# Low parts of the last quad on GpSimd, and the loads of batch five moved, in a fused attention and two-layer mixing kernel

## The chip, the cores and the metric

The kernel runs on one core of a Trainium2 chip. The metric is the device time of one execution in microseconds (us). Engine names are those of the profile: PE (TensorE matmuls), PEld (its weight loads), ACT (ScalarE), DVE (VectorE), POOL (GpSimd), SP (SyncE, which only issues DMAs here). ACTq and SPq are the DMA queues of ACT and SP.

## What is computed

Batch 8, 8 heads, 576 tokens, head size 64, 32 memories per head; then two pairs of dense layers, over tokens (576 to 256 to 576) and over channels (512 to 1536 to 512).

```python
a = exp(phi - max(phi, axis=2)); a = a / (sum(a, axis=2) + 1e-9)
k_m = einsum('bhsm,bhsd->bhmd', a, k)
v_m = einsum('bhsm,bhsd->bhmd', a, v)
scores = q @ k_m.T / sqrt(64); scores = scores - max(scores)
attn = exp(scores); attn = attn / (sum(attn) + 1e-9)
x = concat_heads(attn @ v_m)                 # 8 x 576 x 512
h = relu(x.T @ w_tok1) @ w_tok2
u = x + h.T
out = u + relu(u @ w_ch1) @ w_ch2
```

## The kernel before

**Channel layers.** The 8 x 576 = 4608 rows of u are cut into nine chunks of 512 tokens, and the hidden layer into twelve blocks of 128. An operand is kept as a high part (a rounded cast on ACT) and a low part (what the cast left, a subtraction), and a product of two operands is three matmuls. Chunks 0 to 2 are plain (matmuls L161 and L184). Chunks 3 to 8 do the first layer with seven products of half size instead of eight (class Quarters; products qa and qb at L322, their combined weights loaded as `unit` at L392 on ACT's queue). For each pair of hidden blocks ACT copies products from PSUM into the tile `whole` (L1921), DVE adds them up (L1924), ACT and DVE make the high and low parts (L126, L129), and the second layer (acc, L184) of the pair before fills the gaps between the products. All products of a pair share two PSUM tiles, so the next product into qa waits until ACT has copied the last one out.

**Attention and token layers.** They run in quads, (b, Q) being four heads of batch b (class Quad, L399). A quad loads phi (L407), kv (L412, one buffer) and q (L417), makes the softmax over tokens (phi, with all-reduces over partitions on POOL at L432 and L454), the memories (L467; from (5, 0) on this is issued together with the quad before's scores), the scores (L566), their softmax S, writes S out to DRAM in another layout (`rows`, L663) and reads it back (`raw`, L670 for four full row blocks and L673 for the tail; the buffer is the one that the next quad's q takes). `nat_full` and `nat_tail` split raw into high and low parts (cast on ACT L122, subtraction on DVE L123), `step_A` (Ap, L708) and `step_R` (Rp, L727) are the first token layer, and `step_u` (u, L748) the second one together with attn @ v. For attn, `a_pair` casts a transposed S on ACT (L638) and subtracts on `low_eng` (L639): on POOL for batches 2 and 3, on DVE from batch 4 on. `v_pair` then writes vv on ACT (L652) into the buffer (`aT`) that those subtractions read.

**Order.** Batches 0 and 1 are arranged by a planner; its code is untouched by the change. From then on the order is a table of events written by hand: `at(h, fn)` (L1775) puts a step at a time h counted in half blocks of the channel layers, 24 per chunk, and `run` (L1877) issues it when the loops get there; `quarters` (L1903) has eight such points per pair of hidden blocks, half a unit apart. `starts` (L1779) lists for each quad the times m (memories) and r (scores): (4, 0) has m = 59 and r = 63.5, (4, 1) has 69 and 74, (5, 0) has 79 and 86. Every engine and every DMA queue works strictly in the order in which its instructions are issued.

**The start.** The first lines make an identity matrix on POOL (`make_identity`, masks.py:199 is its AFFINE_SELECT) and a mask (L90 to L95), then a small tile of zeros (L103) that ACT's first activation (L105) reads. PE's first matmuls (L1085) read the identity. Instructions named `ISA` in the order of POOL are of two kinds: those with operands are the all-reduces of L432 and L454, and one without operands stands ahead of every first instruction of another kind (ahead of masks.py:199, ahead of the first L432 after subtractions, ahead of the first L639 or L196 after all-reduces).

Of the kernel before, what the change touches and what calls it, by code (L numbers as in the profile page):

```python
# [28 lines left out]
def kernel(  # L29
# [30 lines left out]
    B, _, _, _, NC, _, D = kv.shape  # L60
# [5 lines left out]
    NF = 2 * w_ch2.shape[0]  # L66
# [1660 lines left out]
    for Q, h0 in ((0, 3), (1, 11)):  # L1727
        qd = quads[1, Q]
        late = 4 if not Q else 0
# [27 lines left out]
    for z in order:  # L1757
        if z.eng == "PE":
# [3 lines left out]
            if gap > 0.3 and z.take:  # L1762

                late = any(y.eng == "SP" and y.ready > z.begin - 0.5 for y in z.after)
# [10 lines left out]
    def at(h, fn, *x, k=0):  # L1775
        events.setdefault((max(h, 0), k), []).append((fn, x))

    JOINT = (4, 1)
    starts = [(2, 0, 24, 24), (2, 1, 34, 34), (3, 0, 38, 44), (3, 1, 49, 54), (4, 0, 59, 63.5), (4, 1, 69, 74)]  # L1779
    while starts[-1][:2] != (B - 1, 1):  # L1780
        b, Q, m, r = starts[-1]
        starts.append((b + Q, 1 - Q, r + 5, r + NF))
    for b, Q, m, r in starts:
        qd = second if b == 2 and not Q else Quad(b, Q)
        fine = b > 2
        if b > 3:
            qd.low_eng = nc.vector
        if qd is not second:
            at(max(m - (13 if JOINT < (b, Q) else 11), 2 * NF), qd.load_phi)
            if fine:  # L1790
                w = 1.5 * ((b, Q) == (5, 0))
                at(m - (6 if (b, Q) == (3, 0) else 8.5 - w), qd.phi_max, k=1)
                w += (b, Q) == (3, 0)
                w -= 1.5 * (JOINT < (b, Q))
                at(m - 4.5 + w, qd.phi_sub)
                at(m - 4 + w, qd.phi_only_exp)
                w += 1.5 * (JOINT < (b, Q))
                at(m - 3.5 + w, qd.phi_sum)
            else:
                at(m - 7, qd.phi_max, k=1)  # L1800
                at(m - 3, qd.phi_exp, k=1)
                at(m - 2, qd.phi_sum, k=1)
            at(loaded + (5 if (b, Q) > (3, 1) else 1), qd.load_kv, k=1)
            at(r - (3 if fine else 4), qd.load_q, k=1)
        joint = JOINT < (b, Q)
        if joint:
            former.follow, loaded = qd, m - 3
        else:
            at(m, qd.step_kv)
            loaded = m  # L1810
        qd.follow, former = None, qd
        at(r + 2, qd.step_s, k=int((b, Q) == (3, 0)))
        if fine:
            late = 0.5 * ((b, Q) == (4, 0))
            for x, fn in (
                (m + 0.5, qd.scales), (m + 1, qd.turn_keys), (m + 1.5, qd.spread_v),
                (m + 3.5, qd.get_keys), (m + 5, qd.v_high), (m + 6, qd.v_low),
                (r + 2.5, qd.S_max), (r + 3, qd.sub_exp), (r + 4, qd.S_sum), (r + 4.5, qd.S_mul),
                (r + 4.5, qd.rows_out), (r + 5, qd.turn_pairs), (r + 8 + late, qd.nat_full),
                (r + 8.5 + late, qd.nat_tail), (r + 9.5 + late, qd.step_A),  # L1820
                (r + 10.5 + late, qd.step_R),
            ):
                at(x, fn)
            at(r + 6, qd.rows_in, "qT", 1)
            for x in range(2):
                at(r + 6 + x / 2, qd.a_pair, x)
                at(r + 7 + x / 2, qd.v_pair, x)
            for x in range(4):
                k = int((b, Q, x) == (3, 1, 0))
                at(r + 12 + x // 2 * 1.5 + x % 2 / 2, qd.step_u, x // 2, x % 2, k=k)  # L1830
            continue
        at(m + 4, qd.values)
        at(m + 1, qd.step_T)
        at(r + 3, qd.sm2)
        at(r + (3 if qd is second else 4), qd.a_pair, 1)
        at(r + 6, qd.nat, k=1)
        at(r + 7, qd.v_pairs)
        at(r + 8, qd.step_A)
        at(r + 9, qd.step_R)
        for x in range(4):  # L1840
            at(r + 10 + x // 2 * (1 if qd is second else 2), qd.step_u, x // 2, x % 2)
    for c in range(2, CHUNKS):
        h = 2 * NF * (c - 1)
        at(h + (9 if c == 2 else 7 if c <= WIN else 1), lambda c=c: mixer(c).take(), k=1)
        if c < WIN:
# [3 lines left out]
        late = (  # L1849
            (-6.5, -3, -2.5, -6.5, -3, -2.5, -3.5, -1, -0.5, -1, -0.5, 0, 0.5)  # L1850
            if c > WIN
            else (-3.5, -3, -2.5, -3.5, -2, -3, -3, -2, -2.5, 0.5, 0.5, 1, 1)
        )
# [217 lines left out]
```

## Time and profile before

| what | value |
|---|---|
| three runs | 772.58, 772.42 and 772.87 us (median 772.58) |
| profiled execution | 773.63 us; its span 771.8 us, so 1.83 us lie outside the span |
| granted clock of TensorE, mean | 0.997 |
| PE busy | 750.7 us (97%), 5159 matmuls |
| DVE, ACT, POOL busy | 469.4 us (61%), 337.3 us (44%), 86.0 us (11%) |
| chain that ended last | PE 79%, DVE 7%, DMA 5%, issue 5% |
| SP's first nine loads | issued from 0.72 to 5.07 us |
| PE's waits from 312 to 330 us | 0.50 at 315.69, 0.54 at 318.64, 0.92 at 322.43, 0.19 at 325.02, 1.94 at 329.53 |

Times inside the profile count from the span's start. A busy PE says only that matmuls follow each other closely; the value in brackets behind an instruction is how long its engine sat idle before it, and which engine's or DMA's end released it. That idle time is shorter than the real gap between two instructions' starts would suggest, since the ends of pipelined matmuls are modelled.

### The profile page before, as it was taken

The numbers are of one execution on the slowest core, as the hardware profiler recorded it, in microseconds if no ns is written. First come the engines' busy times: TensorE is split into PE (matmuls) and PEld (weight loads), VectorE is DVE, ScalarE is ACT, GpSimd is POOL, SyncE is SP. The second block draws the span as 40 slices with busy tenths as digits, with TensorE's granted clock in tenths as the row PEclk, the third lists the DMA queues.
The fourth block names the chain that finished last, engine by engine and source line by source line (L and its number), as shares of the span: only waits on it lengthen the run. The fifth ranks groups of instructions, "written<-read, shape, count | busy, mean of one in ns | idle before, by whom it ended". The sixth has DMA issues, their size and how long they took to land.

```text
span 771.8 us, 13321 instructions
## 1 busy us (share of the span) xinstructions
PE 750.7 (97%) x5159; PEld 652.5 (85%) x5159; DVE 469.4 (61%) x892; ACT 337.3 (44%) x771; POOL 86.0 (11%) x78
## 2 busy tenths in 40 slices
PE   4999999999999999899999999999999999999998
PEld 4877888787888888779898889898989989889987
DVE  1889895577658666756585648674856245335224
ACT  2789663143323243525363536353635343333331
POOL 0224344010132023000000000000000000000000
PEclk9999999999999999999999999999999999999999
DMA  9756442374743554768486848785767356556651
GB/s 364 273 201 248 117 167 73 110 229 167 227 117 87 233 147 128 220 213 282 135 270 198 279 129 250 233 231 173 207 201 199 119 175 225 175 176 212 198 179 68
DMA packets 90446, 147.34 MB, mean 191 GB/s; under 512 B 41488, under 2 KB 60304, under 8 KB 86160
## 3 DMA queue, kind: packets, MB, share of 16 engines
q1 hardware_dynamic: 69216, 79.77, 31.5%
q10 hardware_dynamic: 21168, 66.73, 27.9%
q8 instruction: 41, 0.67, 0.3%
q14 instruction: 21, 0.17, 0.1%
HBM read 121.57 MB, written 24.90 MB: 190 GB/s over the span
## 4 chain that ended last, share of the span: by engine, by line
PE 79%; DVE 7%; DMA 5%; issue 5%; ACT 2%; POOL 1%; SPq 1%; ACTq 0%; POOLq 0%; DVEq 0%
PE acc L184 32%; PE qa L322 12%; PE qb L322 9%; PE cp L161 8%; PE u L748 7%; PE Ap L708 3%; DMA raw<-rows 2%; PE u L1406 2%; DMA rows<-S 2%; PE sp L566 1%; DMA kv<-in_kv_dram 1%; PE Rp L727 1%; PE sp L467 1%; DMA sums<-c1h 1%; PE end L184 1%
## 5 line engine op out<-in xcount | busy, mean ns | idle before, releaser
L184 PE MATMUL acc<-qhh,c 128*128 128x512 f32 x376 | 146.1, 396 | 0.0
L322 PEld LDWEIGHTS qb<-x,unit 128*128 128x128 f32 x648 | 92.2, 189 | 10.4 <-ACT whole L1921 0.9
L322 PEld LDWEIGHTS qa<-xT,unit 128*128 128x128 f32 x648 | 91.8, 188 | 9.5 <-issue 0.2
L184 PE MATMUL acc<-hh,c 128*128 128x512 f32 x288 | 96.5, 394 | 0.0
L322 PE MATMUL qb<-x,unit 128*128 128x256 f32 x648 | 94.7, 282 | 0.5 <-ACT whole L1921 0.5
L322 PE MATMUL qa<-xT,unit 128*128 128x256 f32 x648 | 94.3, 281 | 0.0
L1924 DVE TENSOR_TENSOR whole<-whole 128x256 f32<-128x256 f32 x72 | 30.4, 422 | 101.9 <-ACT whole L1921 101.7
L184 PEld LDWEIGHTS acc<-qhh,c 128*128 128x128 f32 x376 | 71.0, 189 | 12.4 <-issue 3.7
L1921 ACT COPY whole<-qa 128x256 f32<-128x256 f32 x108 | 40.1, 371 | 88.4 <-PE qa L322 84.8
L184 PE MATMUL acc<-qal,c 128*128 128x512 f32 x276 | 78.2, 394 | 0.0
L184 PE MATMUL acc<-qhl,c 128*128 128x512 f32 x188 | 74.9, 398 | 0.0
L184 PEld LDWEIGHTS acc<-hh,c 128*128 128x128 f32 x288 | 54.1, 188 | 13.9 <-issue 2.5
L184 PE MATMUL acc<-hl,c 128*128 128x512 f32 x144 | 56.2, 390 | 0.0
L1921 ACT COPY whole<-qb 128x256 f32<-128x256 f32 x72 | 26.6, 370 | 62.2 <-PE qb L322 62.2
L161 PE MATMUL cp<-uh,c1h 128*128 128x512 f32 x144 | 51.5, 398 | 0.0
L161 PE MATMUL cp<-ul,c1h 128*128 128x512 f32 x144 | 50.3, 390 | 0.0
L161 PE MATMUL cp<-uh,c1l 128*128 128x512 f32 x144 | 50.3, 390 | 0.0
L184 PEld LDWEIGHTS acc<-qal,c 128*128 128x128 f32 x276 | 46.2, 189 | 4.2
L129 DVE SCALAR_TENSOR_TENSOR hl<-cp,hh 128x512 fp32r<-128x512 f32 x36 | 24.7, 686 | 32.3 <-ACT hh L126 32.2
L129 DVE SCALAR_TENSOR_TENSOR qhl<-whole,qhh 128x256 fp32r<-128x256 f32 x72 | 30.4, 422 | 19.2 <-ACT qhh L126 18.4
L126 ACT ACTIVATE qhh<-whole 128x256 fp32r<-128x256 f32 x72 | 30.2, 419 | 25.6 <-DVE whole L1924 18.0
L184 PEld LDWEIGHTS acc<-qhl,c 128*128 128x128 f32 x188 | 36.1, 192 | 0.7
(239 smaller groups left out, 1431.0 us busy)
## 6 DMA issues: line engine op xcount, KB each, us to landing
unit<-sums ACTq DMA_DIRECT2D x108, 512.0 KB, 4.0
kv<-in_kv_dram SPq DMA_DIRECT2D x12, 1280.0 KB, 7.6
rawc<-in_w_ch_dram SPq DMA_DIRECT2D x12, 1024.0 KB, 7.2
q<-in_q_dram SPq DMA_DIRECT2D x16, 576.0 KB, 6.3
unit<-sums ACTq DMA_DIRECT2D x36, 256.0 KB, 3.4
sums<-sums SPq DMA_DIRECT2D x12, 512.0 KB, 6.2
phi<-in_phi_dram SPq DMA_DIRECT2D x16, 320.0 KB, 5.3
out_dram<-u SPq DMA_DIRECT2D x5, 1024.0 KB, 4.2
```

The costliest lines, as they stand in the source:

```text
L126: nc.scalar.activation(out=h, in_=ps, func=AF.Relu)
L129: nc.vector.scalar_tensor_tensor(out=l, in0=ps, scalar=0.0, in1=f32(h), op0=ALU.max, op1=ALU.subtract)
L161: nc.tensor.matmul(ps, l[:, a, w], r[:, a], start=n == 0, stop=n == len(mm) - 1)
L184: nc.tensor.matmul(ps, l_[f // 2][:, f % 2, a * P : (a + 1) * P], r[:, w], start=f == start and x == 0, stop=f == end - 1 and x == 2,)
L322: nc.tensor.matmul(ps[:, :HW], l, r, start=first and n == 0, stop=n == len(mm) - 1, skip_group_check=not first,)
L467: nc.tensor.matmul(s.kvp[32 * i : 32 * i + 32, : 2 * D], s.pt[:, i, j, :], s.kv[:, :, j, i, :], start=j == 0, stop=j == NC - 1,)
L566: nc.tensor.matmul(s.sp[hf][m, :HALF], s.kb[w, m], s.qT[w, i], start=True, stop=True)
L708: nc.tensor.matmul(ps[:, :TT], a, w, start=x == 0, stop=x == len(mm) - 1)
L748: nc.tensor.matmul(ps[:, :HALF], a, r, start=x == 0, stop=x == len(mm) - 1)
L1406: nc.tensor.matmul(ps[:, :HALF], a, r, start=n == 0, stop=n == len(mm) - 1)
L1921: nc.scalar.copy(out=to, in_=ps[:, :HW])
L1924: nc.vector.tensor_tensor(out=to, in0=x, in1=y, op=ALU.add)
```

## The change

Four edits of the event table:

- In the last quad (7, 1) `low_eng` stays POOL, so its two subtractions of L639 move from DVE to POOL.
- The half unit that put `nat_full`, `nat_tail`, `step_A` and `step_R` of quad (4, 0) later is dropped.
- `load_kv` of quad (5, 0) is issued three units after the memories of (4, 1), not five.
- `load_phi` of batch 5 is issued twelve units ahead of m, not thirteen.

```diff
-        if b > 3:
+        if b > 3 and (b, Q) != (B - 1, 1):
             qd.low_eng = nc.vector
         if qd is not second:
-            at(max(m - (13 if JOINT < (b, Q) else 11), 2 * NF), qd.load_phi)
+            at(max(m - (11 if (b, Q) <= JOINT else 12 if b == 5 else 13), 2 * NF), qd.load_phi)
...
-            at(loaded + (5 if (b, Q) > (3, 1) else 1), qd.load_kv, k=1)
+            at(loaded + (3 if (b, Q) == (5, 0) else 5 if b > 3 else 1), qd.load_kv, k=1)
...
         if fine:
-            late = 0.5 * ((b, Q) == (4, 0))
             for x, fn in (
...
-                (r + 4.5, qd.rows_out), (r + 5, qd.turn_pairs), (r + 8 + late, qd.nat_full),
-                (r + 8.5 + late, qd.nat_tail), (r + 9.5 + late, qd.step_A),
-                (r + 10.5 + late, qd.step_R),
+                (r + 4.5, qd.rows_out), (r + 5, qd.turn_pairs), (r + 8, qd.nat_full),
+                (r + 8.5, qd.nat_tail), (r + 9.5, qd.step_A), (r + 10.5, qd.step_R),
```

On ACT, around the token layer of quad (4, 0), the order before was this (names end in the head group and a running number; `whole<-qa` is the copy that frees the PSUM tile of the products qa):

```order
L652 CAST vv_0_3057<-vh_0_2793 64x128 x4
L392 DMA unit_3072<-sums_1326 128x512
L1921 COPY whole<-qa_3_3071 128x256
L122 CAST nat_0_3081<-raw_0_3011 128x512
L1921 COPY whole<-qb_3_3092 128x256
L122 CAST nat_0_3081<-raw_0_3011 64x128
```

With the change the same place on ACT reads (the copies of `whole` are L1919 now, since two lines are gone):

```order
L652 CAST vv_0_3057<-vh_0_2793 64x128 x4
L122 CAST nat_0_3066<-raw_0_3011 128x512
L392 DMA unit_3075<-sums_1326 128x512
L1919 COPY whole<-qa_3_3074 128x256
L122 CAST nat_0_3066<-raw_0_3011 64x128
L1919 COPY whole<-qb_3_3096 128x256
```

The cast of raw now stands ahead of a load of weights and of the copy that frees qa. On DVE the tail's subtraction moves along: it follows the subtraction of the full blocks directly, where a reduction of phi (L421), a residual addition (L202) and an addition of `whole` stood between them. On PE `step_A` stands one product and one group of second-layer matmuls earlier, and `step_R` one product earlier.

On SP's queue, from the keys of quad (4, 1) to the reading back of its rows, the difference is:

```order
 L519 DMA keys_1_3035<-T_1_3032 32x2x32 x4
 L417 DMA q_1_3064<-in_q_dram 128x1152
-L528 DMA kb_1_3103<-keys_1_3035 64x128 x2
-L412 DMA kv_0_3175<-in_kv_dram 128x2560
+L412 DMA kv_0_3090<-in_kv_dram 128x2560
+L528 DMA kb_1_3105<-keys_1_3035 64x128 x2
 L205 DMA out_dram<-o_2809 128x2048
-L407 DMA phi_1_3368<-in_phi_dram 128x640
-L663 DMA rows_1_3383<-S_1_3278 32x18x32 x4
+L663 DMA rows_1_3381<-S_1_3278 32x18x32 x4
+L407 DMA phi_1_3405<-in_phi_dram 128x640
```

The kv of quad (5, 0) goes ahead of two small loads of keys (kb), directly behind q; the phi of quad (5, 1) goes behind the four stores of rows of quad (4, 1) and so between them and the reading back of raw. The phi of (5, 0) keeps its place in the queue.

At the end of POOL's program the difference is:

```order
 L432 ISA prr_1_5483<-pr_1_5481 128x128
 L454 ISA psr_1_5673<-pr_1_5671 128x128
-L2064 UNCONDITIONAL_BRANCH
-L2064 ISA
+L639 ISA
+L639 TENSOR_TENSOR a_7_1_6291<-aT_1_6289,a_7_1_6291 64x576
+L639 TENSOR_TENSOR a_7_1_6292<-aT_1_6289,a_7_1_6292 64x576
+L2062 UNCONDITIONAL_BRANCH
+L2062 ISA
```

The last work of POOL is two subtractions, where it was an all-reduce, with an `ISA` without operands ahead of them.

## Rows read from the trace of the kernel before

**Rows 1.** Waits: engine and line, what it awaited; us in total, times, longest
```profile
PE pp L1085 <- POOL mask L91: 11.0, 1, 11.0
...
PE sp L467 <- DMA kv<-in_kv_dram: 1.9, 1, 1.9
```

**Rows 2.** Timeline of POOL: start, duration, line, operation, [idle before it, releaser]
```profile
10.66 0.28 POOL masks.py:199 TENSOR_SCALAR_AFFINE_SELECT ident<-ident 128x128 f32<-128x128 f32 x1 [9.74 <-issue]
...
273.79 3.80 POOL L639 TENSOR_TENSOR a<-aT,a 64x576 fp32r<-64x576 f32 x2 [15.46 <-ACT a L638]
...
291.30 5.58 POOL L196 TENSOR_TENSOR o<-uh,ul 128x512 f32<-128x512 f32 x4 [7.13 <-DMA kv<-in_kv_dram]
...
534.13 1.07 POOL L454 PARTITION_ALL_REDUCE psr<-pr  x1 [13.56 <-DMA unit<-sums]
```

**Rows 3.** Timeline of PE, the start
```profile
11.00 6.34 PE L1085 MATMUL pp<-ident 128*128 128x128 f32 x30 [11.00 <-POOL mask L91]
...
21.04 0.77 PE L1252 MATMUL kp<-kv,pt 128*32 128x64 f32 x40
```

**Rows 4.** Timeline of PE around quad (4,0)
```profile
312.21 0.87 PE L322 MATMUL qb<-x,unit 128*128 128x256 f32 x6
...
313.62 0.87 PE L322 MATMUL qa<-xT,unit 128*128 128x256 f32 x6
...
315.69 0.98 PE L322 MATMUL qb<-x,unit 128*128 128x256 f32 x6 [0.50 <-ACT whole L1921]
...
326.36 0.30 PE L748 MATMUL u<-a,vv 128*128 128x288 f32 x1
...
327.29 0.29 PE L748 MATMUL u<-w2h,Rl 128*128 128x288 f32 x1
...
329.53 1.30 PE L467 MATMUL sp<-kv,phi 128*32 128x128 f32 x40 [1.94 <-DMA kv<-in_kv_dram]
```

**Rows 5.** Timeline of ACT around quad (4,0)
```profile
311.95 0.37 ACT L1921 COPY whole<-qa 128x256 f32<-128x256 f32 x1
...
314.74 0.62 ACT L122 CAST nat<-raw 128x512 fp32r<-128x512 f32 x1 [2.42 <-DMA raw<-rows]
...
325.73 0.74 ACT L445 ACTIVATE phi<-phi 128x640 f32<-128x640 f32 x1 [0.91 <-DVE phi L435]
```

**Rows 6.** Timeline of SP's queue around quads (4,0) and (4,1)
```profile
318.61 0.35 SPq L417 DMA_DIRECT2D q<-in_q_dram  x1
...
320.34 0.53 SPq L412 DMA_DIRECT2D kv<-in_kv_dram  x1
...
344.28 2.34 SPq L663 DMA_DIRECT2D rows<-S  x4
```

**Rows 7.** Stretches of 2 us: busy time by engine, PEclk, DMA share, GB/s
```profile
330.00:332.00 2.00, 2.00 (x49) 0.89 (x40) 0.00 (x0) 0.00 (x0) 0.00 (x0) 0.69 1.01 416
...
332.00:334.00 2.00, 2.00 (x7) 1.71 (x8) 0.85 (x2) 0.00 (x0) 0.00 (x0) 0.50 0.55 208
```

**Rows 8.** Timeline of SP's queue, the start
```profile
2.10 0.43 SPq L1270 DMA_DIRECT2D kv<-in_kv_dram  x1
```

**Rows 9.** DMA issues, 0 to 24 us: KB each, median us to landing
```profile
kv<-in_kv_dram SPq DMA_DIRECT2D x2, 640.0 KB, 9.2
```

**Rows 10.** Timeline of DVE: quads (4,0), (4,1) and (7,1)
```profile
318.30 0.28 DVE L123 TENSOR_TENSOR nat<-raw,nat 64x128 fp32r<-64x128 f32 x1
...
355.33 1.35 DVE L421 TENSOR_REDUCE pr<-phi 128x128 f32<-128x640 f32 x1
...
589.42 0.75 DVE L639 TENSOR_TENSOR a<-aT,a 64x576 fp32r<-64x576 f32 x1 [1.32 <-ACT a L638]
```

**Rows 11.** The line that loads kv (L412), all twelve loads
```profile
DMA to landing us min/median/max: 5.5/7.6/9.1
```

**Rows 12.** Timeline of ACT, last quad (7,1)
```profile
591.97 0.59 ACT L652 CAST vv<-vh 64x128 fp32r<-64x128 f32 x2
```

**Rows 13.** The chain of waits, 300 to 345 us: start, us, what
```profile
309.65 5.06 DMA raw<-rows
```

## The prediction, made before the run

> **What bounds the kernel now.** I read the waits of the whole run first. PE is busy nearly throughout, so an edit is worth something only where PE itself stands still or runs slower. Two such places lie near the change. The first is the start: PE waits 11.0 us for POOL's mask [rows 1], and POOL's timeline shows why. Its first AFFINE_SELECT begins at 10.66 after 9.74 us in which POOL waited for nothing that the profile shows ("issue") [rows 2]; PE begins at 11.00 [rows 3]. The second is the memories of quad (5, 0): PE waits 1.94 us for kv [rows 1] before 329.53 [rows 4]. The timeline before that shows a row of shorter waits for ACT's copies and for nat; ACT waited 2.42 us for raw before the nat cast at 314.74 [rows 5], and SP issued q at 318.61 and kv only at 320.34 [rows 6]. Right after the wait the stretches 330 to 332 and 332 to 334 have a granted clock of 0.69 and 0.50, the latter being the lower of the clock's two levels, 1.2 GHz [rows 7].
>
> **The change part by part.** The sum is made against the profiled execution, 773.63 us (span 771.8 and 1.83 around it), which is 1.05 above the median of the runs, 772.58; I take the savings off both.
>
> *Last quad's subtractions, at the far end of the program: what POOL leaves behind.* The same unexplained gap appears inside the run. POOL goes from all-reduces back to tensor operations at 291.30 after 7.13 us of idle [rows 2], with a load of kv as releaser, which that addition does not read; I read it so that a change of the kind of operation costs POOL 7 us, and that at the start it asks for the tensor kind once more and loses 9.74. The last work of POOL before is an all-reduce at 534.13 [rows 2]; with the change it is a subtraction, the kind that the next execution begins with. If POOL keeps between executions what it last held, the next start finds it in place. Then POOL could do its AFFINE_SELECT about 9.7 sooner and PE begin at 1.4 instead of 11.0. Not all of it need arrive: the first kv is issued at 2.10 [rows 8] and lands 9.2 later [rows 9], at 11.3, while PE uses it at 21.04 [rows 3], which would be 11.4 with a gain of 9.6. That just fits, and the other early loads have a little more room. I take **-9.1**, bounds -9.6 and -7.5 (two us of late loads), if the gap goes at all. If POOL loads anew at every start, this term is 0; no row here shows what an execution finds in place, since inside the run nothing is ever asked for twice without another kind between. The Trainium skill (GPSIMD Engine Reference, section 2.1) says that the first call to a freshly loaded GpSimd kernel pays an instruction load of about 6 us with no visible instruction. The trace agrees in kind, but its gap at the start is 9.74, and the measurement decides; with 6 the term would be -5.4 and the predicted time 3.7 us higher.
>
> *The same two subtractions in place.* On DVE one takes 0.75, and the first starts at 589.42 [rows 10]; on POOL a pair took 3.80 [rows 2]. Started at 589.42 it ends at 593.22, while ACT writes vv at 591.97 [rows 12], into the buffer that they read; so ACT is 1.25 late, and behind vv in its queue stand the copies that free PE's PSUM tiles. The change of kind itself (7 us by the row above) falls in the more than 50 us that POOL has free after 534.13: the pair at 273.79 followed 15.46 idle us and was released by its ACT cast [rows 2], not by a load. ACT's slack takes up part; I take **+0.4**, bounds 0 and +1.25. What DVE saves, 1.5, lies beside PE's work and is worth nothing.
>
> *The token layer of (4, 0), half a unit sooner.* The nat cast now stands on ACT ahead of the copy at 311.95 [rows 5] that frees qa, and raw lets it begin only at 314.74. So the second qa product, which ran at 313.62, must wait: behind the cast the copy of qb let PE go on at 315.69 [rows 4], 0.95 after the cast's start, and I give the qa product the same start. New wait: 2.07. In return the waits behind it go. From the product at 313.62 to the end of the second u group (327.29, plus one step of 0.13, so 327.42) PE took 13.80. The work in it: six products and two groups of three second-layer matmuls (a product and a group take 1.41 together, 312.21 to 313.62, so eight times 0.705 = 5.64); 14 of Ap and 6 of Rp, each a sixth of a product, 0.12 (2.36); 16 of u at 0.133 (326.36 to 327.29 is seven steps; 2.13) [rows 4]. Together 10.13, so 3.67 were gaps. With the change raw's tail, Al and Ah are ready before PE wants them; I keep 0.3 for the low part of R, whose product now comes earlier by less than what stands behind it. Saving 3.67 - 2.07 - 0.3 = **-1.3** (bounds -0.7, and -1.6 if raw lands a little sooner, since the unit load behind the cast no longer shares with it).
>
> *kv two units sooner.* q takes raw's buffer, so SP cannot issue it until the tail's subtraction on DVE ends, 318.58 [rows 10]; it went at 318.61, kv 1.73 behind it after two kb loads [rows 6]. Now the subtraction follows that of the full blocks and ends near 316.3, q goes at 316.35 and kv 0.4 later, 3.5 sooner. Kv took 9.1 to land, the longest of twelve loads whose median is 7.6 [rows 11]; at 9.1 it lands at 325.9, and PE's second u group ends near 326.1. The wait of 1.94 goes; what is late next is the exponential of phi, which ended at 326.47 on ACT [rows 5]. Taken: 1.94 - 0.4 = **-1.5** (bounds -1.9 and -0.7, kv sharing with q for 1.2 longer). The kb loads, now behind kv, are wanted 1.3 later, after the memories' matmuls.
>
> *The clock.* The two slow stretches lost 2 x 0.31 + 2 x 0.50 = 1.62 [rows 7]. They followed 3.67 of gaps and the wait of 1.94. If the wait goes, so should the fall; but the new wait of 2.07 is as long, and the clock may fall there instead. One chance in four: **-1.2**, bounds -1.62 and 0.
>
> *phi of (5, 1) behind the rows of (4, 1).* It is wanted by the reduction at 355.33 [rows 10]; behind the row stores at 344.28 [rows 6], and an issue time of 2.34, it has 8.7 to land. It delays raw's issue by at most one issue. **+0.2**, bounds 0 and +0.5.
>
> Sum: -9.1 + 0.4 - 1.3 - 1.5 - 1.2 + 0.2 = -12.5. The profiled execution would be 761.1, the median **760.1**.
>
> **The rivals.**
> 1. *The start loads anew every time.* Then the term of 9.1 falls away and -3.4 remain: **769.2**. For it: the idle time at the start could belong to every start, and no row shows it missing. Against it: at the start it is as long as a change of kind inside the run, which the kernel before has to make there and the changed one has not. Chance 0.33.
> 2. *As rival 1, and batch 4 gives little.* The clock falls in the new wait (no saving of 1.2), kv lands 1.2 late, and the subtractions hold ACT up at the full 1.25: -1.3 - 0.7 + 1.25 + 0.2 = -0.55, **772.0**: no change that a measurement can tell. Chance 0.07.
> 3. *Slower, by ACT's order.* As rival 1, and raw lands later than it did. ACT cannot free qa before the nat cast, so each us that raw is late is one of PE's, and q and kv move with it. With the clock fallen -2.2 remain, so raw decides from 3.7 us on beyond its 5.06 [rows 13]: landing after 8.8 it makes the kernel slower by 1.5. At 10 us the time is **775.3**. For it: kv's loads in the same queue spread from 5.5 to 9.1 [rows 11]. Against it: raw is issued at the same point behind the same transfers, and nothing joins it. Chance 0.05.
>
> **How the numbers follow.** Forecast 0.55, rivals 0.33, 0.07 and 0.05. The two ways of the start are 9 us apart and both likely, so the range spans them: from 758.0 (the best bounds of start and batch 4, 14.7 less, rounded) to 771.0, which takes in rival 1 with kv and the subtractions at their worse bounds (+1.65, so 770.8); the forecast's own range is 758.0 to 764.5. About 0.2% (1.5 us) is what a measurement of this kernel can tell from no change. Faster by more: the forecast and rival 1, 0.88; within: rival 2, 0.07; slower: rival 3, 0.05.
>
> **What would show it.** Start: POOL's AFFINE_SELECT near 1 us and PE's first matmul near 1.4, or again 10.7 and 11.0, which is rival 1. Batch 4: a PE wait of about 2 us for ACT's copy of qa, in times of before near 315.7; none for nat or Al; SP's kv about 3.5 sooner, no PE wait over 0.5 for it, and no stretch under a clock of 0.9 behind it. Last quad: ACT's vv released by POOL, up to 1.25 late. The prediction is wrong if the start loses only part of its gap, if kv is still waited for by over 1.2, or if the clock falls in the new wait.

## The result, and the profile after

| | before | with the change |
|---|---|---|
| median of six runs | 772.73 us (771.69 to 776.05) | 760.46 us (757.09 to 762.2) |
| ratio | | 0.983 (95% interval 0.9801 to 0.986) |
| profiled execution, its span | 773.63, 771.8 us | 757.09, 755.3 us |
| PE busy, POOL busy | 750.7, 86.0 us | 747.7, 89.2 us |
| granted clock, mean | 0.997 | 1.0 |

The kernel is 12.3 us faster by the medians. The two profiled executions are further apart, 16.5 us, because the one of the change was the fastest of its six runs and the one of before lies 0.9 us above its median; which part of the 16.5 is the change's and which is that execution's the experiments have to say.

POOL's timeline of the changed kernel, at the start and at the end (columns as in [rows 2]):

```profile
0.72 0.20 POOL masks.py:197 MEMSET ident<- 128x128 f32 x1 [0.29 <-POOLq L2047]
1.22 0.29 POOL masks.py:199 TENSOR_SCALAR_AFFINE_SELECT ident<-ident 128x128 f32<-128x128 f32 x1 [0.30 <-POOL ident masks.py:197]
...
517.58 1.07 POOL L454 PARTITION_ALL_REDUCE psr<-pr  x1 [13.46 <-DVE pr L421]
572.98 3.00 POOL L639 TENSOR_TENSOR a<-aT,a 64x576 fp32r<-64x576 f32 x2 [54.33 <-ACT a L638]
```

The AFFINE_SELECT that began at 10.66 [rows 2] begins at 1.22, and the 9.74 us of "issue" ahead of it are 0.30, the end of the MEMSET that it needs. POOL's last instructions are the pair of subtractions at 572.98; they took 3.00 us for both and were released by ACT's cast. The `ISA` without operands ahead of the AFFINE_SELECT is issued in both kernels (the trace calls it MODIFY_POOL_CONFIG; the last two numbers before the form are the starts of the first and the last one), first in the kernel before, then in the changed one:

```profile
masks.py:199 POOLq MODIFY_POOL_CONFIG  x2: 11/11/11, 0.9 to 1.0; - x2
```

```profile
masks.py:199 POOLq MODIFY_POOL_CONFIG  x2: 11/14/16, 1.1 to 1.1; - x2
```

So the program asks for its kind of operation at the start either way; what differs is whether 9.74 us follow. PE's timeline follows suit (10.81 is the instruction that was at 21.04 [rows 3]):

```profile
1.57 5.54 PE L1085 MATMUL pp<-ident 128*128 128x128 f32 x30 [1.57 <-POOL mask L91]
...
10.81 0.77 PE L1252 MATMUL kp<-kv,pt 128*32 128x64 f32 x40
```

Around quad (4, 0), PE, ACT and SP's queue of the changed kernel, against [rows 4], [rows 5] and [rows 6]:

```profile
302.87 0.40 PE L184 MATMUL acc<-hh,c 128*128 128x512 f32 x1
...
303.89 0.98 PE L322 MATMUL qa<-xT,unit 128*128 128x256 f32 x6 [0.16 <-ACT whole L1919]
...
315.16 1.30 PE L467 MATMUL sp<-kv,phi 128*32 128x128 f32 x40 [0.43 <-DMA kv<-in_kv_dram]
```

```profile
302.95 0.62 ACT L122 CAST nat<-raw 128x512 fp32r<-128x512 f32 x1 [1.07 <-DMA raw<-rows]
...
303.47 0.37 ACT L1919 COPY whole<-qa 128x256 f32<-128x256 f32 x1
...
313.55 0.74 ACT L445 ACTIVATE phi<-phi 128x640 f32<-128x640 f32 x1 [0.38 <-DVE phi L435]
```

```profile
299.44 0.38 SPq L670 DMA_DIRECT2D raw<-rows  x1
...
304.63 0.35 SPq L417 DMA_DIRECT2D q<-in_q_dram  x1
305.03 0.43 SPq L412 DMA_DIRECT2D kv<-in_kv_dram  x1
```

The second qa product waits, as the order of ACT said it would, but little: the acc group at 302.87 takes 0.70, so the product could have begun at 303.57 and began at 303.89. Raw had landed 3.5 us after its issue at 299.44, not 5.06 [rows 13]. Kv is issued 0.40 behind q, and PE waits 0.43 us for it at 315.16 where it waited 1.94. The stretches behind that wait, against [rows 7]:

```profile
316.00:318.00 2.00, 2.00 (x40) 1.20 (x30) 0.80 (x2) 0.00 (x0) 0.00 (x0) 1.00 0.95 384
318.00:320.00 2.00, 2.00 (x17) 1.87 (x16) 0.83 (x3) 0.37 (x1) 0.00 (x0) 1.00 0.33 89
```

No fall of the clock. In the last quad ACT's vv, now released by POOL, behind the copy of qa, in the changed kernel (vv of before is in [rows 12]):

```profile
574.71 0.37 ACT L1919 COPY whole<-qa 128x256 f32<-128x256 f32 x1 [0.34 <-PE qa L322]
...
576.01 0.61 ACT L652 CAST vv<-vh 64x128 fp32r<-64x128 f32 x2 [0.49 <-POOL a L639]
```

and that copy in the kernel before:

```profile
591.25 0.37 ACT L1921 COPY whole<-qa 128x256 f32<-128x256 f32 x1 [0.34 <-PE qa L322]
```

### The profile page after: what moved, and what is told of

It reads as the page before. It is cut to its first block, busy times and chain, and to the rows that moved or that the text cites. A ratio compares the mean times of both kernels' runs of the same rounds, so it can differ in the third digit from the quotient of the medians.

```text
span 755.3 us, 13322 instructions
## 1 busy us (share of the span) xinstructions
PE 747.7 (99%) x5159; PEld 650.8 (86%) x5159; DVE 468.9 (62%) x890; ACT 337.7 (45%) x771; POOL 89.2 (12%) x80
## 4 chain that ended last, share of the span: by engine, by line
PE 81%; DVE 7%; DMA 5%; issue 2%; ACT 2%; POOL 1%; SPq 1%; ACTq 0%; POOLq 0%; DVEq 0%
PE acc L184 33%; PE qa L322 13%; PE qb L322 10%; PE cp L161 8%; PE u L748 7%; PE Ap L708 3%; PE u L1406 2%; DMA kv<-in_kv_dram 1%; DMA k<-in_kv_dram 1%; PE sp L566 1%; PE Rp L727 1%; PE sp L467 1%; DMA raw<-rows 1%; DMA rows<-S 1%; DMA sums<-c1h 1%
## 5 line engine op out<-in xcount | busy, mean ns | idle before, releaser
L1919 ACT COPY whole<-qa 128x256 f32<-128x256 f32 x108 | 40.2, 372 | 88.1 <-PE qa L322 88.0
L1919 ACT COPY whole<-qb 128x256 f32<-128x256 f32 x72 | 26.7, 371 | 58.9 <-PE qb L322 58.9
```

Of the source, the lines that this page charges most:

```text
L1919: nc.scalar.copy(out=to, in_=ps[:, :HW])
```

## The experiments

Twelve kernels were run, each timed in five rounds against the kernel before, whose medians in the three groups of runs were 771.8, 772.76 and 772.33 us. Since single executions of one kernel differ by as much as 8 us, I also read each profile by stretches: PE's 5159 matmuls are the same in every kernel, so numbering them by their start gives stretches that can be compared. In the kernel before, matmul 600 starts at 89.51 us, 2000 at 311.16, 2165 at 335.60 (behind the memories and scores of quad (4, 0) to (5, 0)), 2400 at 371.39 (behind the token layer of (4, 1)), and 4000 to 4200 run from 583.97 to 614.48 (the last quad's token layer). Landing times are DMA issues' times from issue to landing. All columns are in us; those behind the median come from one profiled execution of each kernel, whose time can lie some us off the median.

| kernel | median us | PE's first matmul | 2000 to 2165 | 2165 to 2400 | 4000 to 4200 | raw (4,0) lands | raw (4,1) lands |
|---|---|---|---|---|---|---|---|
| before | 772.73 | 11.00 | 24.45 | 35.79 | 30.51 | 5.1 | 2.9 |
| the change | 760.46 | 1.57 | 18.61 | 35.90 | 30.51 | 3.5 | 2.8 |
| e1_lows_only | 762.52 | 1.57 | 20.35 | 35.80 | 30.51 | 3.4 | 2.7 |
| e2_no_lows | 768.64 | 11.37 | 19.94 | 35.80 | 30.51 | 3.8 | 2.6 |
| e3_end_reduce | 769.77 | 12.05 | 18.80 | 36.11 | 30.51 | 3.6 | 4.0 |
| e4_touch | 760.91 | 1.56 | 19.04 | 37.84 | 30.49 | 3.7 | 3.9 |
| e5_no_nat | 760.27 | 1.56 | 21.53 | 35.80 | 30.51 | 4.9 | 3.4 |
| e6_no_kv | 760.28 | 1.56 | 18.20 | 39.35 | 30.51 | 3.5 | 3.9 |
| e7_again | 759.68 | 1.56 | 18.60 | 40.49 | 30.51 | 3.9 | 6.2 |
| e8_copy_first | 762.05 | 1.56 | 19.97 | 40.52 | 30.51 | 4.9 | 6.2 |
| e9_no_phi | 759.41 | 1.56 | 18.52 | 35.79 | 30.51 | 3.7 | 2.8 |
| e10_touch_no_phi | 759.56 | 1.56 | 19.01 | 35.77 | 30.49 | 3.9 | 3.0 |
| e11_kv_only | 762.56 | 1.56 | 21.63 | 35.80 | 30.51 | 4.9 | 2.8 |
| e12_phi_only | 773.98 | 11.27 | 22.42 | 37.72 | 30.51 | 5.0 | 5.0 |

### The start: what POOL held last

**The last quad's edit alone**, in the kernel before:

```diff
-        if b > 3:
+        if b > 3 and (b, Q) != (B - 1, 1):
             qd.low_eng = nc.vector
```

> The kernel before with only the last quad's two subtractions moved to GpSimd. Theory (GpSimd keeps between executions the kind of operation that it last ran): the AFFINE_SELECT of the start begins near 1.2 us and PE near 1.6, as in the changed kernel, and the time is about 10 us below the kernel before less 0.4 for ACT held up in the last quad: 763 us (762 to 764). Rival (the short start has another cause, in the other edits or in the order of the build): the gap of 9.7 us is there and the time is 772 to 774 us.

Measured: 762.52 us, ratio 0.9875 (0.9848 to 0.9902), 9.3 us below the kernel before; PE begins at 1.57. The theory holds.

**The change without that edit** (the diff above, reversed):

> The changed kernel with the last quad's two subtractions back on VectorE, so only the three edits around batches 4 and 5. Theory: the last work of GpSimd is an all-reduce again, the start has its gap of 9.7 us, PE begins at 11.0, and what is left is the gain of batch 4: between 2 us (the timed runs) and 5.5 us (the profiled run of the change), so 767 to 771 us. Rival (the start does not depend on the last operation): PE begins near 1.6 and the time is 758 to 761 us.

Measured: 768.64 us, ratio 0.9964 (0.9941 to 0.9986), so 3.2 us for the other three edits. The gap at the start is back, here 10.11 us:

```profile
11.03 0.28 POOL masks.py:199 TENSOR_SCALAR_AFFINE_SELECT ident<-ident 128x128 f32<-128x128 f32 x1 [10.11 <-issue]
```

These two leave open whether it is the last operation or the subtractions themselves.

**One all-reduce more behind the subtractions** tells:

```diff
             s.low_eng.tensor_tensor(out=l, in0=s.aT[own], in1=f32(h), op=ALU.subtract)
+            if p and (s.b, s.Q) == (B - 1, 1):
+                m = sb.tile([P, 4 * M], F32, tag="pr", name="last" + s.n, bufs=3)
+                nc.gpsimd.partition_all_reduce(m, ident, P, RED.max)
```

> The changed kernel with one more all-reduce on GpSimd behind the last quad's two subtractions, into a tile that nobody reads, some 170 us before the end. Theory: only what GpSimd ran last matters; the gap at the start is back at 9.7 us and the time is 10 us above the changed kernel, 770 to 771 us. Rival (it matters that the subtractions of the last quad run on GpSimd at all, or that the kind was used late): the start stays short and the time is that of the changed kernel, 760 to 761 us.

Measured: 769.77 us, ratio 0.9982 (0.9965 to 0.9999). POOL's timeline, start and end:

```profile
11.71 0.28 POOL masks.py:199 TENSOR_SCALAR_AFFINE_SELECT ident<-ident 128x128 f32<-128x128 f32 x1 [10.79 <-issue]
...
585.89 3.00 POOL L639 TENSOR_TENSOR a<-aT,a 64x576 fp32r<-64x576 f32 x2 [54.33 <-ACT a L638]
596.30 0.72 POOL L642 PARTITION_ALL_REDUCE last<-ident  x1 [7.41 <-issue]
```

The subtractions ran on POOL as in the change, one all-reduce came after them at 596.30 (7.41 us behind them, "issue"), 170 us before the end and read by nobody, and the next start has a gap of 10.79 us. So it is what POOL ran last, and an execution finds what the one before it left. In all 14 profiles the start fits what the same kernel ends on; what an execution finds behind another program no run here shows.

**The reverse**, subtractions on DVE and a tiny one on POOL behind the last all-reduce:

```diff
             nc.gpsimd.partition_all_reduce(s.r, m, P, RED.add)
+            if (s.b, s.Q) == (B - 1, 1):
+                x = wp.tile([P, 6], F32, name="scrap")
+                nc.gpsimd.tensor_tensor(out=x, in0=mask[:, :6], in1=mask[:, :6], op=ALU.subtract)
...
-        if b > 3 and (b, Q) != (B - 1, 1):
+        if b > 3:
             qd.low_eng = nc.vector
```

> The changed kernel with the last quad's subtractions back on VectorE, and instead one subtraction of 128x6 on GpSimd right behind its last all-reduce, into a tile that nobody reads. Theory: it is enough that the last operation is of the tensor kind; the start is short (PE near 1.6) and the last quad's ACT is not held up, so 0.3 to 0.5 us below the changed kernel: 760 us. Rival (the subtractions in the last quad cost nothing): the same time as the changed kernel within 0.3 us. Rival (a tiny operation does not load the kind): the time of the run without subtractions, 767 to 771 us.

Measured: 760.91 us, ratio 0.9866 (0.9836 to 0.9897); the start is short:

```profile
1.21 0.29 POOL masks.py:199 TENSOR_SCALAR_AFFINE_SELECT ident<-ident 128x128 f32<-128x128 f32 x1 [0.29 <-POOL ident masks.py:197]
...
523.12 1.07 POOL L454 PARTITION_ALL_REDUCE psr<-pr  x1 [13.61 <-DMA unit<-sums]
530.93 0.27 POOL L457 TENSOR_TENSOR scrap<-mask 128x6 f32<-128x6 f32 x1 [6.75 <-issue]
```

A subtraction of 128x6 is enough. It pays its own change of kind, 6.75 us of "issue" at 530.93, where nobody waits for POOL. The time is the changed kernel's, within the noise, and the stretch of the last quad says the same more sharply: 30.51 us with the subtractions on POOL, 30.49 without. The rival is right that they cost nothing there.

### Batch four: which of the three edits

**The half unit taken back** (kv sooner, phi later and the last quad's edit stay):

```diff
+            late = 0.5 * ((b, Q) == (4, 0))
...
-                (r + 4.5, qd.rows_out), (r + 5, qd.turn_pairs), (r + 8, qd.nat_full),
-                (r + 8.5, qd.nat_tail), (r + 9.5, qd.step_A), (r + 10.5, qd.step_R),
+                (r + 4.5, qd.rows_out), (r + 5, qd.turn_pairs), (r + 8 + late, qd.nat_full),
+                (r + 8.5 + late, qd.nat_tail), (r + 9.5 + late, qd.step_A), (r + 10.5 + late, qd.step_R),
```

> The changed kernel with the token layer of quad (4,0) half a unit later again (the edit of the last quad, kv sooner and phi later stay). Theory (the half unit is worth its own gaps and most of kv's lead, since SP's q waits for the tail's subtraction): PE does not wait for the second qa product, but again for nat and Al; in the trace SP issues kv only 0.4 us behind q, some 2 us later than in the changed kernel against the stretch's start, and PE waits 0.5 to 1.5 us for kv; time 1.5 us above the changed kernel, 762 us. Rival (the new wait for the copy of qa costs what the half unit gives): the time of the changed kernel, 760.5 us, or a little below.

Measured: 760.27 us, ratio 0.9838 (0.9812 to 0.9864): the time does not show the loss that was expected. The profile shows it: the stretch from 2000 to 2165 takes 21.53 us against 18.61, with the waits of before back (the last one is now ended by ACT, 0.14 us after kv landed):

```profile
306.28 0.98 PE L322 MATMUL qb<-x,unit 128*128 128x256 f32 x6 [0.46 <-ACT whole L1920]
...
309.24 0.39 PE L708 MATMUL Ap<-w1h,nat 128*128 128x256 f32 x1 [0.54 <-DVE nat L123]
...
313.03 0.39 PE L727 MATMUL Rp<-vh,Al 128*128 128x256 f32 x1 [0.93 <-DVE Al L123]
...
318.74 1.30 PE L467 MATMUL sp<-kv,phi 128*32 128x128 f32 x40 [0.55 <-ACT rest L765]
```

Why the time does not show it is open: the next stretch, below, took 35.80 us in this profile and 37.7 on the mean of all with phi moved, but what it took in the runs without a profile is not known.

**Kv behind the two loads of keys again:**

```diff
-            at(loaded + (3 if (b, Q) == (5, 0) else 5 if b > 3 else 1), qd.load_kv, k=1)
+            at(loaded + (5 if b > 3 else 1), qd.load_kv, k=1)
```

> The changed kernel with kv of quad (5,0) behind the two loads of keys again. Theory: SP issues q as early as in the changed kernel and kv about 1.1 us later than there (two kb issues), so PE waits about 1 us longer for kv; time 761 to 761.5 us. Rival (kv lands early enough either way, and the exponential of phi ends the wait): no PE wait over 0.5 us for kv and 760.5 us.

Measured: 760.28 us, ratio 0.9844 (0.9815 to 0.9874). SP's queue:

```profile
305.63 0.35 SPq L417 DMA_DIRECT2D q<-in_q_dram  x1
306.15 1.09 SPq L528 DMA_DIRECT2D kb<-keys  x2
307.28 0.58 SPq L412 DMA_DIRECT2D kv<-in_kv_dram  x1
```

Kv goes 1.65 us behind q, and PE does not wait for it: the stretch takes 18.20 us, the shortest of all. Kv landed 7.4 us after its issue here, and 8.1 to 10.7 us where it goes directly behind q (10.0 in the change). The rival is right: two units sooner buys nothing that this run shows once q is early. Nor does it alone: e11_kv_only, below, differs from e1_lows_only in nothing but kv, and the medians are 762.56 and 762.52 us (ratios 0.9876 and 0.9875).

**The change once more:**

> The changed kernel once more, without any edit, for the spread. Theory (the profiled run of the change, 757.1 us, was a lucky one of runs from 757 to 762, since raw landed 3.5 us after its issue there and the early loads were in time): median 760.5 us, and a profile whose wait for the copy of qa differs from the 0.16 us of the first one, with the start short in every run. Rival (the short start is there in some executions only): some runs near 770 us.

Measured: 759.68 us (757.15 to 765.4), ratio 0.9843 (0.9808 to 0.9878); no run near 770. The profiled execution, 762.29 us, is 5.2 us slower than the first one, and 4.6 of that lies in one place that no theory had named, the stretch from 2165 to 2400. ACT, PE and the granted clock there:

```profile
341.66 0.62 ACT L122 CAST nat<-raw 128x512 fp32r<-128x512 f32 x1 [4.18 <-DMA raw<-rows]
```

```profile
342.33 0.39 PE L708 MATMUL Ap<-w1h,nat 128*128 128x256 f32 x1 [2.39 <-ACT nat L122]
```

```profile
342.00:344.00 2.00, 1.45 (x10) 1.24 (x11) 1.64 (x4) 1.42 (x5) 0.00 (x0) 1.00 0.98 415
344.00:346.00 2.00, 2.00 (x10) 1.81 (x9) 1.98 (x4) 0.43 (x2) 0.61 (x1) 0.50 0.94 351
346.00:348.00 2.00, 2.00 (x11) 1.81 (x10) 0.90 (x2) 0.22 (x1) 0.20 (x1) 0.65 1.00 310
```

Raw of quad (4, 1) lands 6.23 us after its issue at 335.41 (the chain's row for it is below), PE waits 2.39 us for its cast, and behind that the clock falls to 0.50, the 1.2 GHz level, as it did in [rows 7] behind the wait for kv.

```profile
335.41 6.23 DMA raw<-rows
```

**The copy that frees qa ahead of the nat casts:**

```diff
+            late = 0.5 * ((b, Q) == (4, 0))
...
-                (r + 4.5, qd.rows_out), (r + 5, qd.turn_pairs), (r + 8, qd.nat_full),
+                (r + 4.5, qd.rows_out), (r + 5, qd.turn_pairs), (r + 8 + late, qd.nat_full),
                 (r + 8.5, qd.nat_tail), (r + 9.5, qd.step_A), (r + 10.5, qd.step_R),
```

> The changed kernel with the nat casts of quad (4,0) on ScalarE behind the copy that frees qa, and the rest of its token layer where the change put it. Theory (in-order ScalarE made the second qa product wait for raw): no PE wait for that copy, and a shorter one for nat at Ap's first matmuls, together 0.3 to 0.7 us below the changed kernel in the stretch when raw is as late as in the profile of before; time 760 us. Rival (the same wait moves to Ap in full): the time of the changed kernel, 760.5 us, within the noise.

Measured: 762.05 us, ratio 0.9861 (0.9833 to 0.9888), and 19.97 us in the stretch: both theories missed. PE no longer waits for the copy, but raw is late again, 4.9 us, and ACT's timeline shows what came along:

```profile
302.04 0.33 ACTq L392 DMA_DIRECT2D unit<-sums  x1
...
303.28 0.37 ACT L1920 COPY whole<-qa 128x256 f32<-128x256 f32 x1
305.98 0.62 ACT L122 CAST nat<-raw 128x512 fp32r<-128x512 f32 x1 [2.33 <-DMA raw<-rows]
```

The load of weights is issued at 302.04, one us behind raw, instead of behind the cast that waits for raw. In the kernels where it stands behind the cast raw lands in 3.5 to 3.9 us (eight profiles); where it stands ahead, in 4.9 to 5.1 us (five profiles) and once in 3.4 (e1_lows_only). In that one the load was issued 1.37 us behind raw, in the five 0.84 to 1.19. So the order on ACT that I had counted as the edit's price may have been part of its gain too. That the load is the cause is not shown: no run moves it alone, and in quad (4, 1), in the five profiles with phi ahead of the rows, it was issued 0.59 to 1.16 us behind raw, and raw landed in 2.7 to 3.0.

### Phi between rows and raw

Of the profiles up to here seven have the moved phi besides the change's own. **Phi of (5, 1) back in its old place:**

```diff
-            at(max(m - (11 if (b, Q) <= JOINT else 12 if b == 5 else 13), 2 * NF), qd.load_phi)
+            at(max(m - (11 if (b, Q) <= JOINT else 13), 2 * NF), qd.load_phi)
```

> The changed kernel with the phi of quad (5,1) back ahead of the row stores of (4,1); the other edits stay. Theory (in the slot between rows and raw, phi's load of 320 KB shares the DMA engines with raw, so raw of (4,1) lands late in some executions: PE waited 1.3 to 2.4 us for its nat cast in four of the seven profiles with the edit, and for less than 0.1 us in the two without it): raw of (4,1) lands about 3 us after its issue, no PE wait over 0.3 us for nat there, and about 1 us below the changed kernel, 759 us. Rival (raw is late for another reason, the shifted stores or unit loads): the wait is there again, and the time of the changed kernel, 760.3 us.

Measured: 759.41 us, ratio 0.9836 (0.9799 to 0.9873), 1.0 below the change and 0.3 below its repeat; the stretch takes 35.79 us and raw lands 2.8 us after its issue:

```profile
338.09 0.62 ACT L122 CAST nat<-raw 128x512 fp32r<-128x512 f32 x1 [0.43 <-DMA raw<-rows]
```

**The same with the tiny subtraction instead of the moved ones** (the diffs of e4_touch and e9_no_phi together):

> Candidate to beat both kernels: the last quad's subtractions on VectorE, the one tiny subtraction on GpSimd behind its last all-reduce, kv and the token layer of (4,0) as in the changed kernel, phi of (5,1) back ahead of the rows. Theory: the short start, no ACT held up in the last quad (0.3 us) and no late raw in quad (4,1) (1 us on the mean): 758.5 to 759 us. Rival (neither costs anything): 760.3 us.

Measured: 759.56 us, ratio 0.9841 (0.9807 to 0.9875). It is level with e9_no_phi; neither can be told from the change in time (760.46 and 759.68 in its two groups of runs), so no version here is shown to beat it.

**Kv and the last quad's edit alone** (the diffs of e5_no_nat and e9_no_phi together):

> The last quad's edit and kv sooner alone: the changed kernel without the half unit of (4,0) and with phi of (5,1) back ahead of the rows. Theory (the half unit is worth some 0.5 to 1 us in the stretch through q and kv): 0.5 to 1 us above the run with only phi moved back, 759.5 to 760 us, and PE waits for Al and nat of (4,0) again. Rival (the half unit is worth nothing): the same time as that run, 759 us.

Measured: 762.56 us, ratio 0.9876 (0.9841 to 0.991); 3.1 us above e9_no_phi, and 3.1 us more in the stretch from 2000 to 2165 (21.63 against 18.52). The intervals of the two ratios overlap, but here the profile and the time agree: with phi in its old place the half unit is worth about 3 us, more than expected. With phi moved (e5_no_nat against the change) the profiles show 2.9 us and the medians nothing, so by time alone its worth is not settled.

**Phi later as the only edit:**

```diff
-            at(max(m - (13 if JOINT < (b, Q) else 11), 2 * NF), qd.load_phi)
+            at(max(m - (11 if (b, Q) <= JOINT else 12 if b == 5 else 13), 2 * NF), qd.load_phi)
```

> The kernel before with the phi of (5,1) behind the row stores of (4,1) as its only edit. Theory (phi in that slot makes raw of (4,1) late in some executions, and takes one load out of the way of kv of (5,0)): kv's wait is shorter than in the profile of before (1.94 us), nat of (4,1) can be waited for by 1 to 2.5 us, and the time is the kernel before's within 1 us, 771.5 to 773.5 us. Rival (it is the later phi that brings kv sooner, and the gain of batch 4 is mostly its): 769.5 to 770.5 us.

Measured: 773.98 us, ratio 1.0019 (0.9997 to 1.0041): a little slower, if anything. PE waits for kv 1.28 us, and for the nat cast of (4, 1) 1.16:

```profile
329.84 1.30 PE L467 MATMUL sp<-kv,phi 128*32 128x128 f32 x40 [1.28 <-DMA kv<-in_kv_dram]
...
354.97 0.39 PE L708 MATMUL Ap<-w1h,nat 128*128 128x256 f32 x1 [1.16 <-ACT nat L122]
```

Taken together: with phi ahead of the rows the stretch from 2165 to 2400 takes 35.77 to 35.80 us in all five profiles, and raw lands in 2.7 to 3.0 us. With phi between rows and raw it takes 35.80 to 40.52 us in nine profiles, 37.7 on the mean, and raw lands in 2.6 to 6.2. Where raw takes 3.9 us or more the stretch is longer in every one of the six. That is the one edit of the four that costs time in the profiles, 1.9 us on the mean, and the two profiles of the change itself lie near its ends: 35.90 and 40.49. In the medians, which are 1.65 us apart for e12_phi_only against before and 1.05 for the change against e9_no_phi, the cost is within the intervals.

The same traces show when raw is late. Where phi lands 1.8 to 2.7 us after raw's issue (e3, e5, e7, e8, e12), raw takes 3.4 to 6.2 us. Where phi lands 0.5 to 0.7 us after it, raw takes 2.6 and 2.8 us in e2 and the change, and 3.9 in e4 and e6, in which a load of weights was issued 0.8 to 0.9 us ahead of raw and not 0.7 to 0.8 us behind it. So phi's place is shown to be the cause; whether raw is slowed by phi's own bytes or by the loads that end up beside it, these runs do not separate.

## Why the prediction was right

The time came out as forecast, 760.46 against 760.1, in the case that had the highest chance. The start, three quarters of the sum, was right in its mechanism. That the total agrees within 0.4 us is luck: the terms were off by 0.4 to 1.7 us (those of quad (4, 0) taken together), in both directions. They stand as follows.

**The start, -9.1.** Right in its mechanism, which e3_end_reduce and e4_touch show, and a little small. PE's first matmul came 9.43 us sooner, and matmul 600 ends the account: 89.51, 89.49, 90.49 and 90.01 us in the four profiles with the gap, 79.93 on the mean of the ten without (78.91 to 80.71), so 9.95 us. It is more than the bound of 9.6 because the gap that is saved is itself 9.7 to 10.8 us: the first matmul comes at 11.42 on the mean of those four and at 1.56 in the ten, 9.86 sooner. The early loads, for which I had kept two us, took nothing back: kv was used at 10.81 in the change without a wait, PE waited for it 0.44 us in e1_lows_only and 0.42 in e11_kv_only, and the only longer wait between 2 and 40 us is 0.94 us for ACT, in e1_lows_only. The idle time that a change of kind costs differs by place, 6.75 us ahead of the 128x6 subtraction and 9.74 to 10.79 at the start, so rival 1's remark that the start is as long as a change inside the run (9.74 against 7.13) did not hold, and why it is longer is open. The Trainium skill (GPSIMD Engine Reference, section 2.1) has about 6 us for the load of a fresh kernel: the 6.75 agrees roughly, the start does not, and the measurement decides.

**The subtractions in place, +0.4.** ACT was held up as said: in the changed kernel it stands idle for 0.49 before vv at 576.01, released by POOL. From the copy of qa ahead of it to vv are 1.30 us (574.71 to 576.01); in the kernel before they were 0.72, from 591.25 to [rows 12]. But PE lost nothing, 30.51 us against 30.51 in the stretch; the slack of ACT took all of it.

**Half a unit sooner, -1.3, and the clock, -1.2.** The mechanism of the half unit is right, the sizes are off in ways that cancel; the clock was not the change's to give. With the half unit the stretch from 2000 to 2165 takes 18.20 to 19.97 us in nine profiles (19.97 is e8_copy_first, with its casts moved), without it 20.35 to 24.45 in five. The new wait was put at 2.07 and measured 0.32 in the profile of the change, since raw landed 1.1 to 1.6 us sooner; I had allowed 0.3 for that. In the eight profiles with that order on ACT, PE's idle time there is 0.16 to 1.07 us. The fall of the clock was a feature of the one profile of before: in the four other profiles without the half unit it did not fall, and none of the waits in the stretch made it fall with it. Of the 51 runs of the kernel before that were timed with the experiments, 35 have a mean granted clock of 1.0, where that fall would leave some 0.998 (an estimate: 1.62 us of 772), and they are no faster (772.0 us on the mean, against 771.8 of the twelve at 0.999). A fall that most executions do not have could be taken off the profiled one, not off the median. So 24.45 us was a long execution of that stretch, and with kv sooner in both the half unit is worth 2.6 us (21.58, the mean of e5_no_nat and e11_kv_only, less 18.93, the mean of the seven profiles with the half unit and kv as in the change), with the clock at 1.00 in all of them.

**Kv sooner, -1.5.** This step failed in part. Kv was issued directly behind q as worked out: counted from raw's landing, 3.5 us sooner than before. But I moved its landing by as much as its issue. It landed 8.1 to 10.7 us after the earlier issue, and in 7.4 when it was issued later (e6_no_kv, one profile), and the 0.43 us that PE still waited in the change were for kv and not, as I had it, for the exponential of phi, which had ended at 314.29. What brings kv in time is q's earlier issue, which is the half unit's doing; the position ahead of two small loads, 1.3 of the 3.5 us, is worth nothing that the profiles or the times show.

**Phi behind the rows, +0.2.** The step that was mis-sized most: I priced one issue and the slack of phi itself, and not what a load of 320 KB in that place does to raw, which is issued behind it and wanted first. Measured 0 to 4.7 us, 1.9 on the mean of nine profiles.

**The sum.** -9.95 for the start, 0 for the subtractions, -3.5 for the stretch of (4, 0) (22.41, the mean of before, e1_lows_only and e12_phi_only, less 18.93) and +1.9 for phi make -11.5; the medians give -12.3, with an interval of some 2 us to either side. The stretches of single profiles make the first sum, so it is rough. The forecast of -12.5 had -4.0 for the stretch of (4, 0) and +0.6 for what turned out as +1.9 and 0.

**The rivals.** Rival 1 would have been right had an execution loaded anew at its start; its number, 769.2, is that of e3_end_reduce (769.77) and e2_no_lows (768.64), which end on an all-reduce. Rival 3's mechanism, raw late and PE with it, did occur, not in quad (4, 0) but in (4, 1), and through another edit.

## What to carry to other kernels

What GpSimd holds at the end of a program is what the next execution of it begins with, as long as executions of it follow each other: if the first operation on GpSimd is of another kind than the last, let a tiny operation of the first kind stand last, where nobody waits. Before a load is put anywhere in a queue, ask which load stands behind it and how soon that one is wanted: a large load between a store and its reading back costs the reader, and its own slack says nothing of that. When single executions differ by more than an edit is worth, compare stretches between the same instructions over all profiles at hand; a long wait in one profile of the kernel before may be that execution's own.

## What the runs showed that I had not expected

- The gap at the start vanishes (0.30 us are left, a wait for the MEMSET) in all ten profiles of kernels that end on a subtraction, and none of their timed runs is above 765.52 us. In the four profiles of kernels that end on an all-reduce it is 9.74 to 10.79 us long, and none of their runs is below 766.53 us.
- The same load can take longer to land where it is issued sooner, so an earlier issue is not an earlier landing by as much: kv took 10.0 us issued early and 7.4 issued 1.65 behind q. Raw of (4, 0) took 3.5 to 3.9 us with the weights' load behind the cast, and 4.9 to 5.1 in five of six profiles with it ahead.
- What the clock does behind a wait is not settled by the wait's length alone: in quad (4, 1) it fell, to 0.50 or 0.55 in a stretch of 2 us, behind waits of 1.28 (e6_no_kv), 2.39 (e7_again) and 2.45 us (e8_copy_first), and stayed at 1.00 behind 1.16 (e12_phi_only) and 1.32 us (e4_touch). Of the 4.7 us that a late raw cost e7_again in that stretch, 2.39 are the wait itself and some 1.7 the fall, an estimate from its two slow stretches of 2 us (2 x 0.50 and 2 x 0.35).
